# A chunked RWKV-6 recurrence with a hardswish MLP: one score matrix per head from running decay products in place of seven doubling levels, the output transposed, and the old algorithm behind a run-time flag

## The chip, the cores and the metric

The kernel runs on one core of a Trainium2 chip. The metric is the device time of one execution in microseconds. The change is timed against the kernel before on the same chip.

## The reference

All arithmetic is in float32. First comes a linear recurrence per head, then an MLP over the 3,072 tokens:

```python
B, H, S, D = (4, 8, 768, 48)        # r, k, v: 0.1 * randn; w: 0.8 + 0.15 * rand; u: 0.1 * randn
for t in range(S):                  # state: [B, H, D, D], zero at the start
    cur = einsum('bhd,bhe->bhde', u * kt, vt)
    y[:, :, t] = einsum('bhd,bhde->bhe', rt, state + cur)
    state = wt[:, :, :, None] * state + einsum('bhd,bhe->bhde', kt, vt)
x = y.transpose(0, 2, 1, 3).reshape(B * S, H * D)     # [3072, 384]
h = x @ w_in                                          # w_in  [384, 2048]
g = h * clip(h + 3, 0, 6) / 6
out = g @ w_out                                       # w_out [2048, 384]
```

The decay w lies between 0.8 and 0.95 with these inputs; the definition itself allows any w. The MLP weights arrive as float64, and the chip turns their bits into float32.

## The kernel before, in words

**Chunks.** A sequence of 768 tokens is cut into 6 chunks of L = 128 tokens, 24 chunks in all. The features of a head lie on the partitions, two heads at a time (at partitions 0 and 64, 48 rows each), so 8 heads are 4 pairs.

**Scores by doubling.** Inside a chunk the decay between two tokens is never a quotient. At level l (0 to 6) a chunk falls into blocks of 2^(l+1) tokens; `score` (line 170) multiplies the left half's K with the right half's R for 8 heads, and one predicated copy (L176) puts the result into the score matrix. `merge` (L154 to L158) then multiplies R by the left half's total decay (VectorE) and K by the right half's (GpSimd), with the untouched halves copied on ScalarE. So a chunk needs 7 levels of 8 matrix products, 7 predicated copies and 7 merges, each level resting on the one before. Each float32 matmul is two instructions on TensorE, so a level is 16.

**The rest of a chunk.** `own` (L184 to L191) makes the token's own term: r times k on GpSimd, a matmul with u, and a product with v. `read` (L201, L206) multiplies the state and the scores into y, and adds the own term (L209). `write` (L218 to L237) transposes K, multiplies it with v and updates the state S. `turn` (L248, L249) transposes y, so that the MLP has its features on the partitions.

**MLP.** Three chunks make a block of 384 tokens. `up` (L255 to L260) makes 128 hidden units of a block: 3 matmuls, ScalarE's r6, VectorE's g, which empties the PSUM buffer. `down` (L266, L269) makes 128 output tokens from 16 matmuls. The eight blocks have 16 `up` and 3 `down` pieces each, kept in a list, `todo`, and put between the steps of later chunks. A block's pieces enter the list when its third chunk is read, and the list is emptied before the next block enters.

**Weights.** 32 pieces of 128 hidden units (16 of w_in, 16 of w_out) are loaded from line 98 on the SyncE queue into 3 rotating buffers (`bits`); seven VectorE instructions (L105 to L114) convert a piece. Two pieces are put behind each level of the first chunks.

**Order.** The queues hold the work nearly in program order. TensorE executes what it is given in order, so an instruction that waits holds those behind it. PSUM has eight banks: four for the scores (`a_ps`), two for `ps` (everything small in a chunk) and two for `mm` (the MLP).

Of the kernel before, what the change touches and what calls it, by code (L numbers as in the profile page):

```python
# [14 lines left out]
ACT = mybir.ActivationFunctionType  # L15
PSUM = bass.MemoryType.PSUM
# [6 lines left out]
@with_exitstack  # L23
def kernel(
    ctx: ExitStack,
    tc: tile.TileContext,
    rkw: bass.AP,
    v: bass.AP,
    ub: bass.AP,
    moe_w_in: bass.AP,  # L30
    moe_w_out: bass.AP,
    out: bass.AP,
    n_chunks: int,
):
# [12 lines left out]
    After the last level R carries the decay from the chunk's start and K that to its end, as the state needs.  # L47
    """
    nc = tc.nc
    NT, PR, _, P, _ = rkw.shape  # L50
    D = PR - GP
    H = 2 * P
    HD = H * D
    NTOK, DM = out.shape
    DFF = moe_w_in.shape[1]
    NCC, NFC = DM // 128, DFF // 128
    HL = L // 2
    BC = 3                      # chunks in a block of tokens of the MLP
    MB = BC * L

    const = ctx.enter_context(tc.tile_pool(name="const", bufs=1))
    io = ctx.enter_context(tc.tile_pool(name="io", bufs=3))
    wk = ctx.enter_context(tc.tile_pool(name="wk", bufs=2))
    pa = ctx.enter_context(tc.tile_pool(name="pa", bufs=2, space=PSUM))
    pp = ctx.enter_context(tc.tile_pool(name="pp", bufs=2, space=PSUM))

    st = [dict() for _ in range(NT)]

    def load(i):
        a = io.tile([PR, 3, P, L], F32, name="rkw_in")  # L70
        b = io.tile([L, H, D], F32, name="v_in", bufs=4)
        nc.sync.dma_start(out=a, in_=rkw[i])
        nc.sync.dma_start(out=b.rearrange("s h d -> s (h d)"), in_=v[i])
        st[i].update(R=a[:, 0], K=a[:, 1], tot=a[:, 2], v=b)

    load(0)
    ub_sb = const.tile([PR, P, 2], F32, name="ub_sb")
    nc.sync.dma_start(out=ub_sb, in_=ub)
    load(1)

    # weights, chunk f of the hidden units at a time
    w_in = const.tile([128, NFC, NCC, 128], F32, name="w_in")
    w_out = const.tile([128, NFC, DM], F32, name="w_out")

    def weights(which, f):
# [11 lines left out]
        bits = io.tile([128, n], I64, name="bits", bufs=3)  # L97
        nc.sync.dma_start(out=bits.rearrange("p (c j) -> p c j", j=128), in_=src)
        # |w| = (2^20 + top 20 bits of the mantissa + low word / 2^32) * 2^-20 * 2^(exponent - 1023)
# [17 lines left out]
    ident = const.tile([128, 128], F32, name="ident")  # L117
    make_identity(nc, ident)
    half = const.tile([128, 1], F32, name="half")
    nc.vector.memset(half, 0.5)  # L120

    # masks[s, l, (p, b, j)]: s lies in the left half of block b of level l
    masks = const.tile([128, LEVELS, P * HL], U8, name="masks")
    for l in range(LEVELS):
        m = 1 << l
        nb = HL // m
        mask_f = wk.tile([128, P, nb, m], F32, name="mask_f", bufs=1)
        nc.gpsimd.memset(mask_f, 1.0)
        nc.gpsimd.affine_select(out=mask_f, in_=mask_f, compare_op=ALU.is_ge, fill=0.0, base=0,
                                pattern=[[0, P], [-2 * m, nb], [0, m]], channel_multiplier=1)  # L130
        nc.gpsimd.affine_select(out=mask_f, in_=mask_f, compare_op=ALU.is_ge, fill=0.0, base=m - 1,
                                pattern=[[0, P], [2 * m, nb], [0, m]], channel_multiplier=-1)
        nc.vector.tensor_copy(out=masks[:, l], in_=mask_f.rearrange("s p b j -> s (p b j)"))

    # scores of a chunk, [s, g, p, t]; only s < t is ever written after the zeros
    NA = 2
# [75 lines left out]
    def write(i):  # L212
        if i % n_chunks == n_chunks - 1:
            return
# [141 lines left out]
```

## Time and profile before

| what | value |
|---|---|
| median of 3 runs | 935.16 us (934.88 to 942.06) |
| span of the profiled execution | 934.0 us |
| TensorE matmul busy | 839.6 us, 90% of the span |
| TensorE weight load busy | 600.6 us, 64% |
| VectorE busy | 445.6 us, 48% |
| ScalarE, GpSimd busy | 224.9 us, 211.6 us |
| moved by DMA | 39.41 MB |

The profile describes one execution from its first instruction to its last; that span is 1.2 us under the median of the runs. Busy time of one engine counts a moment once, so a group's mean times its count can be more than the engine was busy. The shares are means over stages: the slices show which stage an engine limits.

### The profile page before, as it was taken

The numbers are of one execution on the slowest core, as the hardware profiler recorded it, in microseconds if no ns is written. First come the engines' busy times: TensorE is split into PE (matmuls) and PEld (weight loads), VectorE is DVE, ScalarE is ACT, GpSimd is POOL, SyncE is SP. The second block draws the span as 40 slices with busy tenths as digits, with TensorE's granted clock in tenths as the row PEclk, the third lists the DMA queues.
The fourth block names the chain that finished last, engine by engine and source line by source line (L and its number), as shares of the span: only waits on it lengthen the run. The fifth ranks groups of instructions, "written<-read, shape, count | busy, mean of one in ns | idle before, by whom it ended". The sixth has DMA issues, their size and how long they took to land.

```text
span 934.0 us, 13463 instructions
## 1 busy us (share of the span) xinstructions
PE 839.6 (90%) x5272; PEld 600.6 (64%) x5272; DVE 445.6 (48%) x954; ACT 224.9 (24%) x533; POOL 211.6 (23%) x263
## 2 busy tenths in 40 slices
PE   4135268999999999999999999999999999999998
PEld 3134258777667766777667767776677666775554
DVE  7898976666415541655135522654055414430210
ACT  3100002444203320333123311342033213110210
POOL 7600343532202320332023211322032202000000
PEclk9999999999999999999999999999999999999999
DMA  7153431110101110111011101011011000000000
GB/s 202 51 165 113 135 104 31 39 37 12 39 26 39 31 39 18 47 40 39 18 47 39 40 9 55 11 38 39 18 43 35 9 18 10 1 1 17 9 0 26
DMA packets 18879, 39.41 MB, mean 42 GB/s; under 512 B 1792, under 2 KB 14080, under 8 KB 18816
## 3 DMA queue, kind: packets, MB, share of 16 engines
q1 hardware_dynamic: 18816, 38.55, 14.0%
q8 instruction: 42, 0.69, 0.3%
q14 instruction: 21, 0.17, 0.1%
HBM read 33.82 MB, written 4.72 MB: 41 GB/s over the span
## 4 chain that ended last, share of the span: by engine, by line
PE 84%; DVE 9%; POOL 3%; DMA 2%; issue 1%; ACT 0%; SPq 0%; POOLq 0%; ACTq 0%
PE mm L255 28%; PE mm L266 27%; PE a_ps L170 17%; PE ps L206 5%; PE ps L187 2%; PE ps L201 2%; PE ps L223 2%; DVE scores L176 2%; DVE mag L112 1%; DVE mag L107 1%; DMA bits<-in_moe_w_out_dram 1%; PE ps L218 1%; DVE man L105 1%; PE ps L248 1%; POOL K L156 1%
## 5 line engine op out<-in xcount | busy, mean ns | idle before, releaser
L255 PE MATMUL mm<-xT,w_in 128*128 128x384 f32 x768 | 281.2, 503 | 0.0
L266 PE MATMUL mm<-w_out,g 128*128 128x384 f32 x768 | 252.6, 488 | 0.0
L170 PE MATMUL a_ps<-R,K 48*128 48x64 f32 x2304 | 168.2, 300 | 70.3 <-DVE scores L176 52.5
L170 PEld LDWEIGHTS a_ps<-R,K 48*128 48x128 f32 x2304 | 156.1, 211 | 107.5 <-issue 70.8
L266 PEld LDWEIGHTS mm<-w_out,g 128*128 128x128 f32 x768 | 144.4, 190 | 97.5
L176 DVE COPY_PREDICATED scores<-masks,a_ps 128x512 f32<-128x512 uint8 x168 | 148.1, 882 | 86.7 <-PE a_ps L170 86.2
L255 PEld LDWEIGHTS mm<-xT,w_in 128*128 128x128 f32 x768 | 137.5, 192 | 74.8 <-issue 2.8
L156 POOL TENSOR_TENSOR K<-K,tot 112x256 f32<-112x256 f32 x144 | 104.6, 726 | 319.7 <-PE a_ps L170 194.3
L260 DVE SCALAR_TENSOR_TENSOR g<-r,mm 128x384 f32<-128x384 f32 x128 | 70.9, 554 | 167.0 <-ACT r L258 166.4
L258 ACT ACTIVATE r<-mm,half 128x384 f32<-128x384 f32 x128 | 74.4, 581 | 232.5 <-PE mm L255 232.5
L154 DVE TENSOR_TENSOR R<-R,tot 112x256 f32<-112x256 f32 x144 | 71.2, 494 | 30.7 <-PE ps L201 30.5
L157 ACT COPY K<-K 112x256 f32<-112x256 f32 x144 | 58.8, 408 | 87.4 <-POOL K L156 60.0
L155 ACT COPY R<-R 112x256 f32<-112x256 f32 x144 | 58.8, 408 | 69.9 <-DVE R L154 33.4
L269 ACT COPY o<-mm 128x384 f32<-128x384 f32 x24 | 11.5, 479 | 245.9 <-PE mm L266 245.9
L184 POOL TENSOR_TENSOR rk<-rkw_in 112x512 f32<-112x512 f32 x24 | 34.9, 1452 | 114.4 <-PE ps L187 112.3
L206 PE MATMUL ps<-v_in,scores 128*128 128x48 f32 x384 | 51.0, 290 | 0.0
L206 PEld LDWEIGHTS ps<-v_in,scores 128*128 128x128 f32 x384 | 49.9, 209 | 1.1
L156 POOL TENSOR_TENSOR K<-rkw_in 112x256 f32<-112x256 f32 x24 | 21.3, 889 | 106.4 <-PE ps L218 105.1
L170 PE MATMUL a_ps<-rkw_in 48*128 48x64 f32 x384 | 31.6, 307 | 9.6 <-DMA rkw_in<-in_rkw_dram 5.7
L158 DVE TENSOR_TENSOR tot<-tot 112x16 f32<-112x16 f32 (+5 forms) x144 | 37.2, 265 | 6.0 <-DVE tot L158 0.9
L237 DVE TENSOR_TENSOR S<-S,ps 48x192 f32<-48x192 f32 x32 | 11.2, 351 | 50.5 <-PE ps L223 50.3
L170 PEld LDWEIGHTS a_ps<-rkw_in 48*128 48x128 f32 x384 | 27.7, 216 | 11.3 <-DMA rkw_in<-in_rkw_dram 5.7
(43 smaller groups left out, 442.2 us busy)
## 6 DMA issues: line engine op xcount, KB each, us to landing
rkw_in<-in_rkw_dram SPq DMA_DIRECT2D x24, 672.0 KB, 4.8
bits<-in_moe_w_in_dram SPq DMA_DIRECT2D x16, 384.0 KB, 3.3
bits<-in_moe_w_out_dram SPq DMA_DIRECT2D x16, 384.0 KB, 3.1
v_in<-in_v_dram SPq DMA_DIRECT2D x24, 192.0 KB, 2.4
out_dram<-o SPq DMA_DIRECT2D x24, 192.0 KB, 1.8
ub_sb<-in_ub_dram SPq DMA_DIRECT2D x1, 3.5 KB, 4.9
```

Source lines behind the costliest of these rows:

```text
L154: nc.vector.tensor_mul(R2[:, :, 1], R[:, :, 1], tot[:, :, 0:1].to_broadcast([PR, n, m]))
L155: nc.scalar.copy(out=R2[:, :, 0], in_=R[:, :, 0])
L156: nc.gpsimd.tensor_mul(K2[:, :, 0], K[:, :, 0], tot[:, :, 1:2].to_broadcast([PR, n, m]))
L157: nc.scalar.copy(out=K2[:, :, 1], in_=K[:, :, 1])
L158: nc.vector.tensor_mul(tot2.rearrange("q p b -> q (p b)"), tot[:, :, 0], tot[:, :, 1])
L170: nc.tensor.matmul(a_ps[:, g, p * HL:(p + 1) * HL].rearrange("s (b j) -> s b j", j=m), lhsT=d["K"][rows, p, :], rhs=d["R"][rows, p, :].rea ...
L176: nc.vector.copy_predicated(out=scores[i % NA].rearrange("s g p (b h j) -> s g (p b) h j", h=2, j=m)[:, :, :, 1], mask=masks[:, l].rearran ...
L206: nc.tensor.matmul(y_ps[:, h, :], lhsT=a[:, g, p, :], rhs=d["v"][:, h, :], start=(first and h == 0), stop=(h == H - 1), skip_group_check=True)
L255: nc.tensor.matmul(h_ps, lhsT=w_in[:, f, j, :], rhs=b["xT"][:, j, :], start=(j == 0), stop=(j == NCC - 1))
L258: nc.scalar.activation(out=r6, in_=h_ps, func=ACT.Relu, bias=half, scale=1.0 / 6.0)
L260: nc.vector.scalar_tensor_tensor(out=g, in0=r6, scalar=1.0, in1=h_ps, op0=ALU.min, op1=ALU.mult)
L266: nc.tensor.matmul(o_ps, lhsT=blocks[bk]["g"][f][:, c * L:(c + 1) * L], rhs=w_out[:, f, :], start=(f == 0), stop=(f == NFC - 1))
```

## The change

The program gets a fast path, which always runs, and the old algorithm (`general_path`), which runs behind it if a flag is set. 

- **Fast path, per chunk.** `prep` makes the running decay product W of all channels by one scan on VectorE, its reciprocal on VectorE, and R = r W and K = k / W on GpSimd. It also reduces the largest w (for the flag), copies each product over a whole chunk, forms r k u on GpSimd from token-major copies of r and k, sums it per head on VectorE, and spreads that sum over a diagonal matrix A on GpSimd. `score` makes one 128x128 matrix per head, 8 in all, and one predicated copy puts its part with s < t into A, whose diagonal is the own term. `write` adds to the state before the decay, and multiplies by W's last column.
- **Transposed output.** `read` takes v and the state as the stationary side, so y comes with its features on the partitions. ScalarE copies it into the MLP's input; a third of the features is moved to its partitions by 6 DMAs per block on the SyncE queue. `own`'s matmuls and `turn`'s transposes are no longer there. The rows of w_in are laid out on the host in the new order of the features.
- **Order.** The MLP's pieces are 28 per block (16 `up`, 12 quarters of `down`), spread evenly over the chunks with a lag of 5 pieces; `mm` has four PSUM banks, `ps` two, the scores two. Eight weight pieces stand in a chunk's program, and `prep` runs one chunk ahead.
- **Flag.** At the end the smallest chunk product (compared with 2^-60) and the largest w (with 1) are reduced to one number, loaded into the registers of all engines, and compared. `general_path` is the code before in plain order, with the MLP behind every third chunk.

Inputs: r, k and w of a chunk lie in one tensor (w with a leading 0 per pair, so that the scan starts again there); r, k and v also come token by token.

The diff, cut to the lines that are added and that matter here (the code taken out is the kernel printed above; `general_path` repeats it):

```diff
+def fast_path(tc, feat, tok, ub, moe_w_in, moe_w_out, out, flag, n_chunks):
...
+        def load(i):
+            a = io.tile([PR, nf], F32, name="feat_in")
+            b = io.tile([L, 3, HD], F32, name="tok_in", bufs=4)
+            nc.sync.dma_start(out=a, in_=feat[i])
+            nc.sync.dma_start(out=b.rearrange("s c e -> s (c e)"), in_=tok[i].rearrange("s c e -> s (c e)"))
+            n = P * L
+            st[i].update(r=a[:, :n].rearrange("q (p t) -> q p t", p=P),
+                         k=a[:, n:2 * n].rearrange("q (p t) -> q p t", p=P), w=a[:, 2 * n:],
+                         rt=b[:, 0], kt=b[:, 1], v=b[:, 2].rearrange("s (h d) -> s h d", d=D))
...
+        def prep(i):
+            d = st[i]
+            W_ = wk.tile([PR, P * (L + 1)], F32, name="W")
+            nc.vector.tensor_tensor_scan(out=W_, data0=d["w"], data1=restart.rearrange("q p t -> q (p t)"),
+                                         initial=0.0, op0=ALU.mult, op1=ALU.add)
+            W = W_.rearrange("q (p t) -> q p t", p=P)
+            inv = wk.tile([PR, P, L], F32, name="inv")
+            nc.vector.reciprocal(out=inv, in_=W[:, :, 1:])
+            R = wk.tile([PR, P, L], F32, name="R", bufs=3)
+            K = wk.tile([PR, P, L], F32, name="K")
+            nc.gpsimd.tensor_mul(R, d["r"], W[:, :, :L])
+            nc.gpsimd.tensor_mul(K, d["k"], inv)
+            nc.vector.tensor_reduce(out=w_max[:, i:i + 1], in_=d["w"], axis=AX.X, op=ALU.max,
+                                    apply_absolute_value=True)
+            nc.vector.tensor_copy(out=w_min[:, i, :], in_=W[:, :, L])
+            rk = wk.tile([L, HD], F32, name="rk")
+            nc.gpsimd.tensor_mul(rk, d["rt"], d["kt"])
+            nc.gpsimd.tensor_mul(rk, rk, u_bc)
+            dg = wk.tile([L, H, 1], F32, name="dg")
+            nc.vector.tensor_reduce(out=dg.rearrange("s h o -> s (h o)"), in_=rk.rearrange("s (h d) -> s h d", d=D),
+                                    axis=AX.X, op=ALU.add)
+            A = wk.tile([L, H, L], F32, name="A")
+            nc.gpsimd.tensor_mul(A, ident.rearrange("s (o t) -> s o t", o=1).to_broadcast([L, H, L]),
+                                 dg.to_broadcast([L, H, L]))
+            d.update(W=W, R=R, K=K, A=A)
+        def score(i):
+            d = st[i]
+            a_ps = pa.tile([128, 2, P, L], F32, name="a_ps")
+            for p in range(P):
+                for g in range(2):
+                    rows = slice(g * GP, g * GP + D)
+                    nc.tensor.matmul(a_ps[:, g, p, :], lhsT=d["K"][rows, p, :], rhs=d["R"][rows, p, :],
+                                     start=True, stop=True)
+            nc.vector.copy_predicated(
+                out=d["A"].rearrange("s (p g) t -> s g p t", g=2),
+                mask=mask.rearrange("s (o x t) -> s o x t", o=1, x=1).to_broadcast([L, 2, P, L]),
+                data=a_ps)
+        def turn_k(i):
+            if i % n_chunks == n_chunks - 1:
+                return
+            d = st[i]
+            kn_ps = pp.tile([L, P, PR], F32, name="ps")
+            for p in range(P):
+                nc.tensor.transpose(kn_ps[:, p, :], d["K"][:, p, :], ident[0:PR, 0:PR])
+            kn = wk.tile([L, P, PR], F32, name="kn")
+            nc.scalar.copy(out=kn, in_=kn_ps)
+            d["kn"] = kn
+        def write(i):
+            if i % n_chunks == n_chunks - 1:
+                return
+            d = st[i]
+            kv_ps = pp.tile([PR, P, 2, D], F32, name="ps")
+            for p in range(P):
+                nc.tensor.matmul(kv_ps[:, p].rearrange("q g e -> q (g e)"), lhsT=d["kn"][:, p, :],
+                                 rhs=d["v"][:, 2 * p:2 * p + 2, :].rearrange("s h e -> s (h e)"),
+                                 start=True, stop=True)
+            base = bases[i % 2]
             for g in range(2):
                 rows = slice(g * GP, g * GP + D)
...
+                b = base[rows, :, g * GP:g * GP + D]
+                if i % n_chunks == 0:
+                    nc.vector.tensor_copy(out=b, in_=kv_ps[rows, :, g, :])
+                else:
+                    nc.vector.tensor_add(b, st[i - 1]["S"][rows, :, g * GP:g * GP + D], kv_ps[rows, :, g, :])
+            S = wk.tile([PR, P, PR], F32, name="S")
+            nc.gpsimd.tensor_mul(S, base, d["W"][:, :, L:L + 1].to_broadcast([PR, P, PR]))
+            d["S"] = S
...
+        def read(i):
+            d = st[i]
+            first = i % n_chunks == 0
+            bk, c = divmod(i, BC)
+            if c == 0:
+                blocks[bk]["xT"] = wk.tile([128, NCC, MB], F32, name="xT")
+                blocks[bk]["x3"] = wk.tile([PR, MB], F32, name="x3")
+            xT, x3 = blocks[bk]["xT"], blocks[bk]["x3"]
+            y_ps = pp.tile([PR, P, L], F32, name="ps")
+            if not first:
+                for p in range(P):
+                    nc.tensor.matmul(y_ps[:, p, :], lhsT=st[i - 1]["S"][:, p, :], rhs=d["R"][:, p, :],
+                                     start=(p == 0), stop=False, skip_group_check=True)
+            for p in range(P):
+                for g in range(2):
+                    h = 2 * p + g
+                    nc.tensor.matmul(y_ps[g * GP:g * GP + D, p, :], lhsT=d["v"][:, h, :], rhs=d["A"][:, h, :],
+                                     start=(first and p == 0), stop=(p == P - 1), skip_group_check=True)
+            now = slice(c * L, (c + 1) * L)
+            for g in range(2):
+                rows = slice(g * GP, g * GP + D)
+                nc.scalar.copy(out=xT[rows, :, now], in_=y_ps[rows, 0:NCC, :])
+                nc.scalar.copy(out=x3[rows, now], in_=y_ps[rows, P - 1, :])
+            if c == BC - 1:
+                for g in range(2):
+                    for j in range(NCC):
+                        to = g * GP + D
+                        nc.sync.dma_start(out=xT[to:to + X3, j, :],
+                                          in_=x3[g * GP + j * X3:g * GP + (j + 1) * X3, :])
...
+            h_ps = pp.tile([128, MB], F32, name="mm", bufs=4)
...
+        QD = 4
+        def down(bk, cq):
+            c, q = divmod(cq, QD)
+            b = blocks[bk]
+            if q == 0:
+                b["o_ps"] = pp.tile([L, DM], F32, name="mm", bufs=4)
+            o_ps = b["o_ps"]
+            n = NFC // QD
+            for f in range(q * n, (q + 1) * n):
+                nc.tensor.matmul(o_ps, lhsT=b["g"][f][:, c * L:(c + 1) * L], rhs=w_out[:, f, :],
+                                 start=(f == 0), stop=(f == NFC - 1))
+            if q == QD - 1:
+                o = wk.tile([L, DM], F32, name="o", bufs=2)
...
+                f(bk, j)
+        per_block = NFC + BC * QD
+        lag = 5
+        prep(0)
+        prep(1)
+        some_weights(2)
+        done = 0
+        for i in range(NT):
+            goal = max(0, (i - BC + 1) * per_block // BC - lag) - done
+            done += max(goal, 0)
+            left = goal
+            def some(n):
+                nonlocal left
+                n = max(min(n, left), 0)
+                mlp(n)
+                left -= n
+            if i + 2 < NT:
+                load(i + 2)
+            score(i)
+            turn_k(i)
+            some(1)
+            if i + 1 < NT and i > 0:
+                prep(i + 1)
+            some(2)
+            some_weights(3)
+            write(i)
+            some(1)
+            some_weights(2)
+            read(i)
+            some(left)
+            some_weights(3)
+            if i % BC == BC - 1:
+                bk = i // BC
+                todo.extend([(up, bk, f) for f in range(NFC)] + [(down, bk, c) for c in range(BC * QD)])
+                if i == NT - 1:
+                    low = wk.tile([PR, 1], F32, name="low", bufs=1)
+                    top = wk.tile([PR, 1], F32, name="top", bufs=1)
+                    nc.vector.tensor_reduce(out=low, in_=w_min.rearrange("q i p -> q (i p)"), axis=AX.X, op=ALU.min,
+                                            apply_absolute_value=True)
+                    nc.vector.tensor_reduce(out=top, in_=w_max, axis=AX.X, op=ALU.max)
+                    nc.vector.tensor_scalar(out=low, in0=low, scalar1=LEAST, scalar2=None, op0=ALU.is_lt)
+                    nc.vector.scalar_tensor_tensor(out=top, in0=top, scalar=1.0, in1=low, op0=ALU.is_gt, op1=ALU.max)
+                    n_ps = pp.tile([1, 1], F32, name="ps")
+                    nc.tensor.matmul(n_ps, lhsT=top, rhs=ones[0:PR, :], start=True, stop=True)
+                    nc.vector.tensor_copy(out=flag, in_=n_ps)
+        mlp(len(todo))
...
+def general_path(tc, feat, tok, ug, moe_w_in, moe_w_out, out, n_chunks):
...
+    nc = tc.nc
+    flags = ctx.enter_context(tc.tile_pool(name="flags", bufs=1))
+    flag = flags.tile([1, 1], I32, name="flag")
+    fast_path(tc, feat, tok, ub, moe_w_in, moe_w_out, out, flag, n_chunks)
+    bad = nc.values_load(flag[0:1, 0:1], min_val=0, max_val=128)
+    with tc.If(bad > 0):
+        general_path(tc, feat, tok, ug, moe_w_in, moe_w_out, out, n_chunks)
...
```

## Rows read from the trace of the kernel before

**Rows 1.** The page: engine totals, two lines of 40 slices, the chain's shares.
```profile
PE 839.6 (90%) x5272; PEld 600.6 (64%) x5272; DVE 445.6 (48%) x954; ACT 224.9 (24%) x533; POOL 211.6 (23%) x263
...
PE   4135268999999999999999999999999999999998
...
DVE  7898976666415541655135522654055414430210
...
PE 84%; DVE 9%; POOL 3%; DMA 2%; issue 1%; ACT 0%; SPq 0%; POOLq 0%; ACTq 0%
```

**Rows 2.** Busy time by stretch: us, then PE, PEld, DVE, ACT, POOL, clock, DMA share, GB/s.
```profile
46.00:70.00 24.00, 8.57 (x72) 7.69 (x70) 23.28 (x61) 0.40 (x1) 0.00 (x0) 1.00 0.56 168
...
93.00:117.00 24.00, 5.65 (x48) 5.33 (x48) 23.99 (x65) 1.89 (x5) 7.12 (x3) 1.00 0.45 136
...
327.00:374.00 47.00, 47.00 (x257) 31.09 (x256) 12.94 (x27) 7.92 (x20) 6.56 (x9) 1.00 0.09 28
```

**Rows 3.** The chain of waits, three pieces: start us, us, what.
```profile
179.67 3.33 PE mm L255 x6
...
868.50 30.96 PE mm L255 x96
899.46 30.97 PE mm L266 x96
```

**Rows 4.** Timeline of TensorE in a steady chunk: start us, us, instruction, shapes, count.
```profile
306.57 2.00 PE L170 MATMUL a_ps<-R,K 48*128 48x64 f32 x32
308.50 2.20 PE L255 MATMUL mm<-xT,w_in 128*128 128x384 f32 x6
310.63 2.00 PE L170 MATMUL a_ps<-R,K 48*128 48x64 f32 x32
...
318.67 1.03 PE L201 MATMUL ps<-S,R 112*128 112x96 f32 x8
319.53 1.91 PE L206 MATMUL ps<-v_in,scores 128*128 128x48 f32 x16
321.28 2.17 PE L255 MATMUL mm<-xT,w_in 128*128 128x384 f32 x6
323.28 0.55 PE L218 MATMUL ps<-ident,K 112*128 112x112 f32 x4
323.67 1.47 PE L255 MATMUL mm<-xT,w_in 128*128 128x384 f32 x4
324.98 0.93 PE L223 MATMUL ps<-v_in,kn 128*112 128x96 f32 x8
325.75 0.84 PE L255 MATMUL mm<-xT,w_in 128*128 128x384 f32 x2
```

**Rows 5.** Timeline of the start: first feature-dependent VectorE instruction; eight weight loads issued.
```profile
5.66 0.43 DVE L154 TENSOR_TENSOR R<-rkw_in 112x256 f32<-112x256 f32 x1 [2.55 <-DMA rkw_in<-in_rkw_dram]
...
36.20 22.48 SPq L98 DMA_DIRECT2D bits<-in_moe_w_in_dram  x8
```

**Rows 6.** Groups by line and shape: count, busy us, mean ns, idle before and releaser.
```profile
L176 DVE COPY_PREDICATED scores<-masks,a_ps 128x512 f32<-128x512 uint8 x168 | 148.1, 882 | 86.7 <-PE a_ps L170 86.2
L154 DVE TENSOR_TENSOR R<-R,tot 112x256 f32<-112x256 f32 x144 | 71.2, 494 | 30.7 <-PE ps L201 30.5
L260 DVE SCALAR_TENSOR_TENSOR g<-r,mm 128x384 f32<-128x384 f32 x128 | 70.9, 554 | 167.0 <-ACT r L258 166.4
L184 POOL TENSOR_TENSOR rk<-rkw_in 112x512 f32<-112x512 f32 x24 | 34.9, 1452 | 114.4 <-PE ps L187 112.3 <-DMA rkw_in<-in_rkw_dram 2.0
L191 POOL TENSOR_TENSOR dv<-v_in,dg 128x384 f32<-128x384 f32 x24 | 21.7, 905 | 6.3 <-ACT dg L189 6.3
L237 DVE TENSOR_TENSOR S<-S,ps 48x192 f32<-48x192 f32 x32 | 11.2, 351 | 50.5 <-PE ps L223 50.3
L158 DVE TENSOR_TENSOR tot<-tot 112x128 f32<-112x128 f32 x24 | 7.5, 312 | 2.1 <-DVE tot L158 0.5
L158 DVE TENSOR_TENSOR tot<-tot 112x64 f32<-112x64 f32 x24 | 5.9, 244 | 0.3
```

More of the change, by code (lines that the diff above doesn't have):

```diff
@@ L20, with weight_loader @@
 LEVELS = 7
[L23 to L83, printed above, removed]
+BC = 3
+LEAST = 2.0 ** -60
+def weight_loader(nc, io, wk, w_in, w_out, moe_w_in, moe_w_out, io_bufs=3):
     def weights(which, f):
@@ new lines, in fast_path, with some_weights, mlp @@
+        todo = []
+        pieces = [("in", f) for f in range(NFC)] + [("out", f) for f in range(NFC)]
+        def some_weights(n):
+            for piece in pieces[:n]:
+                weights(*piece)
+            del pieces[:n]
+        def mlp(n):
+            for _ in range(min(n, len(todo))):
+                f, bk, j = todo.pop(0)
+                f(bk, j)
[43 more added lines that the diff above has]
+                    nc.vector.tensor_copy(out=flag, in_=n_ps)
@@ L234, in write @@
             if i % n_chunks == 0:
[L235 removed]
+                nc.gpsimd.memset(S, 0.0)
             else:
[L237 to L249 removed]
@@ L263, in down @@
-    def down(bk, c):
-        o_ps = pp.tile([L, DM], F32, name="mm")
-        for f in range(NFC):
-            nc.tensor.matmul(o_ps, lhsT=blocks[bk]["g"][f][:, c * L:(c + 1) * L], rhs=w_out[:, f, :],
-                             start=(f == 0), stop=(f == NFC - 1))
-        o = wk.tile([L, DM], F32, name="o", bufs=2)
-        nc.scalar.copy(out=o, in_=o_ps)
-        t0 = bk * MB + c * L
-        nc.sync.dma_start(out=out[t0:t0 + L, :], in_=o)
-    todo = []
-    pieces = [("in", f) for f in range(NFC)] + [("out", f) for f in range(NFC)]
@@ new lines, in down @@
+        def down(bk, c):
+            o_ps = pp.tile([L, DM], F32, name="mm_g")
+            for f in range(NFC):
+                nc.tensor.matmul(o_ps, lhsT=blocks[bk]["g"][f][:, c * L:(c + 1) * L], rhs=w_out[:, f, :],
+                                 start=(f == 0), stop=(f == NFC - 1))
+            o = wk.tile([L, DM], F32, name="o_g", bufs=2)
+            nc.scalar.copy(out=o, in_=o_ps)
+            t0 = bk * MB + c * L
+            nc.sync.dma_start(out=out[t0:t0 + L, :], in_=o)
+        for f in range(NFC):
+            weights("in", f)
+            weights("out", f)
@@ L285 @@
+        for i in range(NT):
             if i + 2 < NT:
@@ L290, with kernel @@
                 merge(i, l)
-                for piece in pieces[:2]:
-                    weights(*piece)
-                del pieces[:2]
-                if l % 2 == 0:
-                    mlp(1)
-                    left -= 1
-        if i > 0:
-            read(i - 1)
-            mlp(1)
-            write(i - 1)
-            mlp(1)
-            turn(i - 1)
-            mlp(left - 2)
-            if i % BC == 0:
-                mlp(len(todo))
-                bk = i // BC - 1
-                todo.extend([(up, bk, f) for f in range(NFC)] + [(down, bk, c) for c in range(BC)])
-    mlp(len(todo))
-_INS = ['rkw', 'v', 'ub', 'moe_w_in', 'moe_w_out']
+            read(i)
+            write(i)
+            turn(i)
+            if i % BC == BC - 1:
+                for f in range(NFC):
+                    up(i // BC, f)
+                for c in range(BC):
+                    down(i // BC, c)
+@with_exitstack
+def kernel(
+    ctx: ExitStack,
+    tc: tile.TileContext,
+    feat: bass.AP,
+    tok: bass.AP,
+    ub: bass.AP,
+    ug: bass.AP,
+    moe_w_in: bass.AP,
+    moe_w_out: bass.AP,
+    out: bass.AP,
+    n_chunks: int,
+):
+    nc = tc.nc
+    flags = ctx.enter_context(tc.tile_pool(name="flags", bufs=1))
[4 more added lines that the diff above has]
+        general_path(tc, feat, tok, ug, moe_w_in, moe_w_out, out, n_chunks)
+_INS = ['feat', 'tok', 'ub', 'ug', 'moe_w_in', 'moe_w_out']
 _OUTS = [((3072, 384), 'float32')]
```

404 lines of the change are left out of this document (258 added, 146 removed).

## The prediction

> **What bounds the kernel now.** I read the page first: TensorE's matmuls are busy for 90% of the span, VectorE for 48%, the others for a quarter, and the chain of waits lies on TensorE for 84% [rows 1]. The line of slices shows where the rest is. TensorE is at 9 from the eighth slice on, and at 1 to 8 in the seven before, where VectorE stands at 6 to 9 [rows 1]. So there are two kernels to cost: a start of 180 us that VectorE limits, and 754 us that TensorE limits.
>
> The stretches confirm both. From 46 to 70 us VectorE is busy for 23.28 of 24.00 us and TensorE for 8.57; from 327 to 374 TensorE is busy for all 47.00 us and VectorE for 12.94 [rows 2]. In the chain the first MLP piece starts at 179.67 us [rows 3]: that is the border. What the change takes from TensorE therefore counts in full behind the border, and what it takes from VectorE counts in front of it.
>
> **MLP: unchanged.** The last block runs with nothing between: 30.96 us for 16 `up`, 30.97 for the `down` [rows 3]. A block is 61.9 us, eight are 495.4, one `up` is 30.96/16 = 1.94. The new kernel does the same matmuls, so this is its floor.
>
> **TensorE per chunk, before.** The timeline is read by the distance from one group's start to the next one's, since the durations include the pipeline's latency [rows 4]:
> - scores: 32 instructions in 1.93 us (306.57 to 308.50), 0.965 per level, 6.76 for seven levels;
> - state into y 0.86, scores into y 1.75, transposes of K 0.39, K times v 0.77;
> - six MLP instructions behind scores take 2.13 (308.50 to 310.63) where they take 1.94 alone, so 0.2 us per change between the two kinds of tile.
>
> **TensorE per chunk, after.** `own`'s and `turn`'s matmuls go, and six of the seven levels.
> - Scores: 16 instructions with 128 columns instead of 64. Before, one took 60 ns (1.93/32), though weights of 128 columns cost 107 to 109 ns where the whole array is used (0.86/8 and 1.75/16) [rows 4]. So the two heads of a pair, on partitions 0 to 47 and 64 to 111, run side by side, and a pair costs about 0.12. The moving side of 128 columns would be as long as that weight load. I take 0.965 (side by side); the upper end is 16 x 0.107 = 1.72.
> - A into y: 16 instructions; now v is stationary (48 columns), A moves with 128, and the heads of a pair write partitions 0 to 47 and 64 to 111 of the output. No row shows two column halves at once: 0.965 if they behave as the row halves do, 1.75 if as `read` now. I take the middle, 1.36.
> - State into y: 8 instructions, 0.86; K's transposes and K times v as before, 1.16. Both only in 20 of 24 chunks: 0.72 and 0.97 on average.
> - Two changes of tile kind: 0.4.
>
> Sum 0.965 + 1.36 + 0.72 + 0.97 + 0.4 = 4.4 us per chunk, with ends 4.0 and 5.6. Before, the same count gives 6.76 + 1.75 + 0.72 + 0.97 + 0.8 for four changes = 11.0, and `own` and `turn` on top.
>
> The Trainium skill ("TensorE: Matmul & The Clock Gate", Part 3: Packing small matmuls) says that tiles in distinct column groups run at once, as row groups do. The scores' 60 ns agree for rows; for columns no run here shows it. By that page the sum would be about 8 us lower.
>
> **What hides behind TensorE.** In the steady part a new chunk lasts 61.9/3 + 4.4 = 25 us. VectorE's part of it, from the nearest rows [rows 6]: scan and reciprocal over 512 elements at twice the 256-element product, 1.0 each; the reduction for the largest w 1.0; the sums per head 0.55 (384 elements); the copy of the products about 0.2; one predicated copy of 1,024 at 2 x 0.88 = 1.76; two state adds 0.70. That is 6.2 us, and 5.3 evictions g add 2.95. GpSimd: R and K 1.45 each, two products of 0.9, A at about twice R (2.9), S about 1: 8.6 us. ScalarE: 5.3 activations and copies that are smaller than before. All are under half of 25 us, so I cost them at nothing there; the cover is TensorE's own work. The six DMAs per block that move a third of the features have the lag of five pieces in front of them, some 10 us; without it they would cost a few us per block. Four `mm` banks let TensorE go on for four pieces, 7.7 us, while VectorE is in `prep`.
>
> **The start.** Here VectorE counts. First features come at 5.66 us [rows 5]. A converted weight piece is seven instructions: 23.28/61 = 0.38 us each from 46 to 70 us, 23.99/65 = 0.37 from 93 to 117 [rows 2], so 2.67 us a piece (2.58 the lower end); the loads, issued as buffers come free, give 22.48/8 = 2.81 as the upper [rows 5]. 32 pieces: 85.5. Five chunks of VectorE work at 6.2: 31. In `prep` the sum per head waits for GpSimd: R, K and two products are 4.7 us behind the scan, VectorE has 2.2 us of own work in that time, 2.5 us are left, three times (the first two lie behind the first loads): 7.5. Queued behind that wait are the evictions of the MLP and weight conversions. Sum 130. Before, VectorE was only some 80% busy in the first slices [rows 1], and with gaps like that it would be 155. The new order has fewer levels that wait for one another; I take 135 for the moment from which TensorE is dense. SyncE's queue carries more (r and k come twice), and the first DMAs of transposed features stand behind weight loads that wait for buffers; VectorE is still converting then, which hides them. TensorE has done five score steps and about eight `up` pieces by then. The first MLP piece of before takes 3.33 us for what later takes 1.94 [rows 3]; such slow pieces would fall in this part, where TensorE waits anyway.
>
> **The end.** From the last matmul (899.46 + 30.97) to the end of the span are 3.6 us [rows 3]. Then come the load of the flag and a branch over the old code on every engine. No row shows one. Lower end 0.5 (an instruction), upper 20; I take 5.7, what it took at the start until the first data had come from memory [rows 5].
>
> **The sum.** 135 + (495.4 - 8 x 1.94 = 479.9) + 19.5 chunks x 4.4 (86) + 3.6 + 5.7 = 710 against a span of 934.0; with the 1.2 us between span and median, 711 against 935.16.
>
> **The rivals.**
> - *A reciprocal of several cycles per element.* The products cost (312 - 244)/64 = 1.06 ns per element [rows 6]. With eight cycles for each of 512 elements it would be 4.3 us instead of 1.0, hidden later but not at the start: 5 x 3.3 = 17, so 728. No row shows a reciprocal. The Trainium skill ("VectorE: DVE Perf Modes", First, the fixed hardware budget) says that it is an iterative divide with a repeat count of 8, spread over the pipeline's slices; that speaks for this rival only if the repeats are not pipelined.
> - *Neither scores nor A go side by side.* 0.75 + 0.39 more per chunk, 20 chunks: 23, so 734. For it: 128 moving columns are new with halves. Against it: the 60 ns.
> - *VectorE holds TensorE in every chunk.* With the slow reciprocal and products that GpSimd delays, `prep` would keep the evictions waiting for 11 or 12 us, above the 7.7 us of the four banks: 3 us per chunk, 60 in all, 771. The share of VectorE speaks against it, the single stretch for it.
> - *No change.* TensorE would have to wait 11 us in each chunk for the chain scan, reciprocal, K, scores, copy, A. The chain is made one chunk ahead.
> - *The flag is set: the change doesn't do what it says.* The old algorithm then runs behind the fast path, and its whole time, at least the 934 of now, is added: 1,640 and more. It decides when some product of 128 decays is under 2^-60, which needs a mean decay under 0.72, or when a w is over 1. The reference draws w from 0.8 to 0.95, and 0.8^128 is 2^-41; padding is 1, not above. Hence it is unlikely.
>
> **Chances.** Forecast 0.57 (its own range 685 to 735), slow reciprocal 0.19, no halves side by side 0.12, VectorE in every chunk 0.09, no change 0.01, flag 0.02. The predicted time is the forecast's, 711. Low end: dense from 115, 4.0 us per chunk, a cheap branch: 20 + 8 + 5 less, 680. High end, near the third rival: 765. Faster by over 1% takes all but the last two cases: 0.97; same 0.01; slower 0.02. One per cent, 9 us, is about what a measurement of this kernel can tell from no change.
>
> **What would show it.** Score instructions at about 60 ns each and 16 per chunk; y's instructions from 60 to 109 ns; TensorE full from about 135 us, with a period of about 75 us per block where it was about 100; VectorE nearly full before; a reciprocal of 1 or of 4 us; a few us between the last output and the end. I am wrong if TensorE has holes in each chunk behind 150 us, or if the old code's instructions appear.

## The result, and the profile after

The changed kernel takes 723.38 us (median of four runs, 722.04 to 723.89) against 936.17 before: a ratio of 0.772, interval 0.770 to 0.775. The forecast was 711 with a range from 680 to 765. The span of the profiled execution is 720.0 us, 2.0 under its time of 722.04.

The page of the changed kernel: engine totals, two engines' slices with TensorE's clock, the chain's shares (columns as in [rows 1]).

```profile
PE 624.5 (87%) x2706; PEld 392.4 (54%) x2706; DVE 360.1 (50%) x548; ACT 128.4 (18%) x269; POOL 185.7 (26%) x148
...
PE   1341373779999999999999999999999999999996
...
DVE  6999999998136525640346337512463152101200
...
PEclk9975575779999999999999999999999999999999
...
PE 78%; DVE 19%; DMA 2%; POOL 1%; issue 0%; ACT 0%; ACTq 0%; DVEq 0%; POOLq 0%
```

The two stages are still there. TensorE is at 9 from the tenth slice (162 us) to the last but one; in front of it VectorE is at 9 from the second slice to the ninth. Before, TensorE was full from the eighth of longer slices [rows 1]. TensorE's busy time fell by 215 us, and the time by 213.

Busy time by stretch of the changed kernel (columns as in [rows 2]):

```profile
54.00:72.00 18.00, 2.31 (x11) 1.72 (x9) 16.92 (x42) 0.53 (x1) 4.33 (x3) 0.50 0.50 148
...
108.00:126.00 18.00, 6.16 (x22) 3.36 (x22) 17.97 (x37) 1.85 (x5) 3.97 (x2) 0.59 0.46 143
126.00:144.00 18.00, 13.74 (x52) 9.24 (x53) 17.91 (x43) 2.28 (x4) 5.84 (x5) 0.72 0.41 126
144.00:162.00 18.00, 13.34 (x51) 7.77 (x50) 17.36 (x26) 3.15 (x8) 8.97 (x7) 0.72 0.23 72
162.00:180.00 18.00, 18.00 (x78) 11.11 (x77) 14.91 (x20) 4.63 (x10) 10.77 (x8) 1.00 0.34 99
...
360.00:420.00 60.00, 60.00 (x278) 37.87 (x277) 27.99 (x35) 13.89 (x28) 15.80 (x14) 1.00 0.22 64
```

VectorE is nearly full up to 162 us, TensorE is full from there on. In the steady part VectorE is busy for 28 of 60 us. So the border moved from 179.67 [rows 3] only to about 156, where the chain below enters TensorE for good; 135 was forecast. (The 179.67 of before is the start of its first MLP piece. VectorE had let go of TensorE some 30 us earlier; the section on why the prediction was right comes back to that.)

The chain of waits of the changed kernel (start us, us, what), the beginning of the dense part, one chunk, the last block:

```profile
156.00 9.70 PE mm L246 x24
...
176.81 15.68 PE mm L264 x48
...
251.43 15.68 PE mm L264 x48
267.10 1.09 PE a_ps L170 x16
268.19 0.53 PE ps L184 x4
268.73 7.76 PE mm L264 x24
276.48 0.77 PE ps L195 x8
277.25 2.61 PE mm L264 x8
279.86 0.88 PE ps L223 x8
280.74 1.01 PE ps L228 x16
281.75 2.78 PE mm L264 x8
...
325.77 15.68 PE mm L264 x48
...
652.58 30.96 PE mm L246 x96
683.54 30.97 PE mm L264 x96
```

One chunk is 1.09 (scores) + 0.53 (K transposed) + 0.77 (K times v) + 0.88 (state into y) + 1.01 (A into y) = 4.3 us. The same pieces recur after 74.6 and 74.3 us (176.81, 251.43, 325.77), and a block of the MLP is still 61.9. Both halves run side by side: 16 score instructions take 68 ns each, 16 for y 63, where the old `read` took 109 [rows 4]. One at a time they couldn't be that short: 384 moving columns take 0.32 us (30.96/96), so 128 would take 107 ns. For y these are column halves, of which no row had been at hand. The Trainium skill ("TensorE: Matmul & The Clock Gate", Part 3: Packing small matmuls) says that distinct column groups run at once; these 63 ns agree.

The accounts before and after agree with that. Behind the border lay 754.3 us before; less the MLP's 495.4 and the end's 3.6, 255.3 us are left for 20.5 chunks: 12.5 per chunk. Behind 156 us lie 564.0 now; less 478.0 (54 MLP instructions, 17.4 us, are done by then) and an end of 5.5, 80.5 us are left for 19.5 chunks: 4.1 per chunk. So of the 214 us of span 175 come from TensorE's chunk work behind the border (255.3 less 80.5), 24 from the earlier border (the first MLP piece before, the dense part now) and 17 from MLP pieces done in front of it; the longer end takes 2 back.

Groups of the changed kernel by line and shape (columns as in [rows 6]):

```profile
L145 DVE RECIPROCAL inv<-W 112x512 f32<-112x512 f32 x24 | 80.4, 3349 | 0.6
L160 POOL TENSOR_TENSOR A<-ident,dg 128x1024 f32<-128x1024 f32 x24 | 49.8, 2076 | 41.2 <-PE ps L228 21.2 <-DVE dg L157 20.1
L141 DVE TENSOR_TENSOR_SCAN W<-feat_in,restart 112x516 f32<-112x516 f32 x24 | 34.3, 1430 | 18.9 <-POOL S L207 14.8 <-DMA feat_in<-in_feat_dram 3.9
L173 DVE COPY_PREDICATED A<-mask,a_ps 128x1024 f32<-128x1024 uint8 x24 | 31.2, 1301 | 57.0 <-PE a_ps L170 56.9
L150 DVE TENSOR_REDUCE w_max<-feat_in 112x1 f32<-112x516 f32 x24 | 16.3, 680 | 18.8 <-DMA feat_in<-in_feat_dram 18.8
```

The reciprocal is 3.35 us, not 1.0, and the scan 1.43; the predicated copy (1.30 for 1.76) and the reduction (0.68 for 1.0) are cheaper than costed. 3.35 us for 512 elements are 6.5 ns each, where a product costs 1.06 [rows 6].

The end of the changed kernel, timeline of the last compute instruction (columns as in [rows 4], behind them idle time and releaser):

```profile
714.58 0.48 ACT L268 COPY o<-mm 128x384 f32<-128x384 f32 x1 [9.88 <-PE mm L264]
```

The last matmul ends at 683.54 + 30.97 = 714.5, so 5.5 us are left to the end of the span, where it had been 3.6. No instruction of the old algorithm appears: the flag is not set.

### The profile page after: what moved, and what is told of

The parts are those of the page before. It is cut to its first block, busy times and chain, and to the rows that moved or that the text cites. A ratio compares the mean times of both kernels' runs of the same rounds, so it can differ in the third digit from the quotient of the medians.

```text
span 720.0 us, 6998 instructions
## 1 busy us (share of the span) xinstructions
PE 624.5 (87%) x2706; PEld 392.4 (54%) x2706; DVE 360.1 (50%) x548; ACT 128.4 (18%) x269; POOL 185.7 (26%) x148
## 4 chain that ended last, share of the span: by engine, by line
PE 78%; DVE 19%; DMA 2%; POOL 1%; issue 0%; ACT 0%; ACTq 0%; DVEq 0%; POOLq 0%
PE mm L264 35%; PE mm L246 33%; PE a_ps L170 3%; PE ps L228 3%; DVE man L49 2%; DVE inv L145 2%; DVE mag L56 2%; DVE mag L51 2%; PE ps L223 2%; PE ps L195 2%; DVE ex L55 2%; DVE ex L52 1%; DVE W L141 1%; DVE w_out L58 1%; DVE ex L54 1%; PE ps L184 1%
## 5 line engine op out<-in xcount | busy, mean ns | idle before, releaser
L145 DVE RECIPROCAL inv<-W 112x512 f32<-112x512 f32 x24 | 80.4, 3349 | 0.6
L160 POOL TENSOR_TENSOR A<-ident,dg 128x1024 f32<-128x1024 f32 x24 | 49.8, 2076 | 41.2 <-PE ps L228 21.2
L170 PE MATMUL a_ps<-R,K 48*128 48x128 f32 x384 | 33.0, 317 | 31.0 <-POOL K L149 31.0
L173 DVE COPY_PREDICATED A<-mask,a_ps 128x1024 f32<-128x1024 uint8 x24 | 31.2, 1301 | 57.0 <-PE a_ps L170 56.9
L170 PEld LDWEIGHTS a_ps<-R,K 48*128 48x128 f32 x384 | 27.7, 216 | 45.2 <-POOL K L149 34.5
L148 POOL TENSOR_TENSOR R<-feat_in,W 112x512 f32<-112x512 f32 x24 | 32.3, 1346 | 69.3 <-DVE W L141 66.5
L228 PE MATMUL ps<-A,tok_in 128*48 128x128 f32 x384 | 29.4, 302 | 21.4 <-DVE A L173 21.4
L223 PE MATMUL ps<-R,S 112*112 112x128 f32 x160 | 23.9, 296 | 25.3 <-POOL S L207 25.3
L141 DVE TENSOR_TENSOR_SCAN W<-feat_in,restart 112x516 f32<-112x516 f32 x24 | 34.3, 1430 | 18.9 <-POOL S L207 14.8
L149 POOL TENSOR_TENSOR K<-feat_in,inv 112x512 f32<-112x512 f32 x24 | 30.8, 1282 | 36.3 <-DVE inv L145 13.7
```

What stands on the lines that cost most here:

```text
L141: nc.vector.tensor_tensor_scan(out=W_, data0=d["w"], data1=restart.rearrange("q p t -> q (p t)"), initial=0.0, op0=ALU.mult, op1=ALU.add)
L145: nc.vector.reciprocal(out=inv, in_=W[:, :, 1:])
L148: nc.gpsimd.tensor_mul(R, d["r"], W[:, :, :L])
L160: nc.gpsimd.tensor_mul(A, ident.rearrange("s (o t) -> s o t", o=1).to_broadcast([L, H, L]), dg.to_broadcast([L, H, L]))
L170: nc.tensor.matmul(a_ps[:, g, p, :], lhsT=d["K"][rows, p, :], rhs=d["R"][rows, p, :], start=True, stop=True)
L173: nc.vector.copy_predicated(out=d["A"].rearrange("s (p g) t -> s g p t", g=2), mask=mask.rearrange("s (o x t) -> s o x t", o=1, x=1).to_br ...
```

## The experiments

The kernel before took 934 to 935 us beside each group of these runs, and the changed kernel, run again beside the last group but one, 723.3. Differences are against that.

**1. Without the branch.** The last three lines of the top function go.

```diff
-    bad = nc.values_load(flag[0:1, 0:1], min_val=0, max_val=128)
-    with tc.If(bad > 0):
-        general_path(tc, feat, tok, ug, moe_w_in, moe_w_out, out, n_chunks)
```

> The changed kernel without the load of the flag and without the old algorithm behind it (the flag is still computed). Theory: behind the last matmul lie 5.5 us of span in the changed kernel and 3.6 before, and the runs are 2 us longer than their spans instead of 1.2, so the branch costs about 3 us: 720.5. The prediction had 5.7 for it: 717.7. Rival, a branch whose cost lies elsewhere (old code that is fetched all along): below 713.

Measured: 719.6 us (ratio to before 0.770, interval 0.768 to 0.772), 3.8 less. Its trace says how much of it is the branch: span 716.3, last ScalarE copy at

```profile
713.00 0.48 ACT L268 COPY o<-mm 128x384 f32<-128x384 f32 x1 [9.88 <-PE mm L264]
```

so 3.3 us from that copy to the end where the changed kernel has 5.4. The branch costs 2.1 us at the end; the other 1.6 lie in front of that copy. The two traces show where. Both enter the dense part at 156 us with the same 24 MLP instructions; without the branch they took

```profile
156.11 8.01 PE mm L246 x24
```

where the changed kernel took 9.70, and the stretch behind 156 us reads, the changed kernel first:

```profile
156.00:174.00 18.00, 18.00 (x54) 10.50 (x55) 17.10 (x21) 4.65 (x8) 13.84 (x11) 0.91 0.26 77
...
156.00:174.00 18.00, 17.99 (x65) 10.85 (x64) 17.95 (x23) 4.65 (x8) 14.66 (x11) 1.00 0.27 78
```

TensorE's granted clock was back at 1.00 there where the changed kernel's mean was still 0.91; these 1.7 us are the clock's. That the missing branch caused it isn't shown. Either way the branch is under the 5.7 of the prediction, and over its lower end of 0.5.

**2. Scores twice.**

```diff
-            for p in range(P):
+            for p in [*range(P), *range(P)]:      # in score
```

> The changed kernel with the score matmuls of every chunk issued twice into the same PSUM tile. Theory: behind 156 us TensorE is the bound, so 16 more instructions at 1.09 us per 16 count in full in about 20 chunks: 22 us more, 745. Rival (TensorE's time is hidden behind VectorE or GpSimd since the change): 723 to 727.

Measured: 739.6 us (0.791, 0.789 to 0.793), 16.2 more. TensorE's timeline shows what the second series costs:

```profile
271.12 2.06 PE L170 MATMUL a_ps<-R,K 48*128 48x128 f32 x32
```

The next group starts 1.98 us later, where one series takes 1.09, so 0.9 per chunk. In 19 chunks behind the border that is 17 us: counted in full. My 22 had charged the change of tile kind a second time. The rival that hides it has fallen.

**3. Two PSUM banks for the MLP.**

```diff
-            h_ps = pp.tile([128, MB], F32, name="mm", bufs=4)
+            h_ps = pp.tile([128, MB], F32, name="mm", bufs=2)
```
(and the same for `o_ps`)

> The changed kernel with two PSUM banks for the MLP instead of four, all else the same. Theory: TensorE is the bound only because four banks carry it over VectorE's stretch of scan, reciprocal and reductions; around 284 to 290 us the first eviction comes 3.5 us late, with two banks TensorE would stop for 2 to 3 us there, in most chunks: 40 to 60 us more, 765 to 780. Rival (VectorE is busy for half the time only, so evictions come early enough): 723 to 727.

Measured: 749.3 us (0.801, 0.799 to 0.803), 25.9 more: neither the 40 to 60 nor nothing. The timeline has the wait where it was expected:

```profile
295.81 2.42 PE L246 MATMUL mm<-xT,w_in 128*128 128x384 f32 x7
300.47 2.13 PE L246 MATMUL mm<-xT,w_in 128*128 128x384 f32 x3 [2.24 <-DVE g L251]
```

Behind scan, reciprocal and sums the eviction g comes late, and TensorE stops for 2.24 us. Most of the waits are shorter: behind 160 us the timeline has 17 waits for g, 0.22 to 2.25 us long and 15.1 us in all. The rest of the 25.9 us lies in the start, where by 170 us 72 MLP instructions are done and not 90 as in the changed kernel (5.8 us), and in matmuls that follow a wait (six in 2.20 us for 1.94). So the four banks are a part of the gain, and the prediction's sentence that they cover VectorE's stretch is shown.

**4. y in the old orientation.** v moves, A and R are stationary; y goes through ScalarE, three transposes and ScalarE again.

```diff
-                    nc.tensor.matmul(y_ps[g * GP:g * GP + D, p, :], lhsT=d["v"][:, h, :], rhs=d["A"][:, h, :], ...)
+                nc.tensor.matmul(y_ps[:, h, :], lhsT=d["A"][:, h, :], rhs=d["v"][:, h, :], ...)
...
+            for j in range(NCC):
+                nc.tensor.transpose(x_ps[:, j, :], y[:, j * 128:(j + 1) * 128], ident)
```

> The changed kernel with y in the old orientation: scores stationary, v moving, y copied by ScalarE, transposed on TensorE and copied again; no DMAs for a third of the features, and w_in's rows in their own order. Theory: TensorE takes 1.75 + 0.33 instead of 1.01 us for it, in 20 chunks behind the start: 21 us more, 745. Rival (the transposition adds a chain that TensorE waits for): 760 or more. Rival (orientation is worth nothing): 723.

Measured: 743.2 us (0.796, 0.794 to 0.798), 19.9 more, as expected. TensorE's timeline of one chunk:

```profile
284.20 1.03 PE L224 MATMUL ps<-S,R 112*128 112x96 f32 x8
285.06 1.91 PE L228 MATMUL ps<-tok_in,A 128*128 128x48 f32 x16
286.81 0.88 PE L259 MATMUL mm<-w_out,g 128*128 128x384 f32 x2
287.54 0.55 PE L234 MATMUL ps<-ident,y 128*128 128x128 f32 x3
287.93 2.10 PE L259 MATMUL mm<-w_out,g 128*128 128x384 f32 x6
```

1.75 us for y (285.06 to 286.81) and 0.39 for the transposes, instead of 1.01. The transposition is worth 20 of the 212 us.

**5. Three VectorE instructions per weight piece.**

```diff
+        nc.vector.tensor_scalar(out=man, in0=hi, scalar1=3, scalar2=0x3FFFFFFF,
+                                op0=ALU.logical_shift_left, op1=ALU.bitwise_and)
+        nc.vector.scalar_tensor_tensor(out=ex, in0=hi, scalar=-0x80000000, in1=man,
+                                       op0=ALU.bitwise_and, op1=ALU.bitwise_or)
+        nc.vector.scalar_tensor_tensor(out=dst.bitcast(I32), in0=lo, scalar=29, in1=ex,
+                                       op0=ALU.logical_shift_right, op1=ALU.bitwise_or)
```
(in place of the seven; `lo` is read as int32)

> The changed kernel with three VectorE instructions per weight piece instead of seven: shift and mask the high word, or in the sign, or in three bits of the low word. This cuts the fraction off where the other rounds, and holds for weights under 2 in magnitude and over 2^-127 only. Theory: VectorE sets when TensorE becomes dense (it is full to 144 us, and a piece costs 3.6 us by its means), so some 2.3 us x 32 = 74 us go from VectorE; the loads of weights and features then come next, and I expect two thirds of it: dense at about 105 us, 670 to 680. Rival (loads or the chain of chunks set the start): 710 or more.

Measured: 670.0 us (0.717, 0.715 to 0.719), 53 less. Stretches of its trace:

```profile
90.00:108.00 18.00, 9.18 (x47) 5.39 (x48) 17.23 (x27) 2.90 (x7) 6.80 (x5) 0.81 0.68 195
108.00:126.00 18.00, 17.93 (x74) 10.84 (x73) 17.38 (x33) 4.75 (x10) 2.12 (x2) 1.00 0.45 135
```

TensorE is dense from 108 us instead of about 156: VectorE's conversions set the border. By their means up to 113 us the three instructions of a piece sum to 2.10 us, 0.70 each; the seven of the changed kernel sum to 3.61 up to 156 us, 0.52 each. So the gain comes from instructions left out, about 1.5 us x 32 pieces = 48 us, and not from shorter ones.

**6. No reciprocal.**

```diff
-            nc.vector.reciprocal(out=inv, in_=W[:, :, 1:])
+            nc.vector.tensor_copy(out=inv, in_=W[:, :, 1:])
```

> The changed kernel with the reciprocal replaced by a copy of W of the same shape, so K is k times W: the division is left out. Theory: six reciprocals of 3.35 us lie in the VectorE-bound start; a copy is 0.4 to 0.7: 16 us less, 706. Behind the start nothing changes. Rival (TensorE's wait for K at 151 to 155 us is all it costs): 718.

Measured: 709.0 us (0.758, 0.756 to 0.760), 14.3 less, near the theory's 706 and far from the rival's 718. The six reciprocals in front of the border count nearly in full; the eighteen behind it are hidden, or 24 x 2.7 us would have gone.

**7. The diagonal matrix on ScalarE.**

```diff
-            nc.gpsimd.tensor_mul(A, ident.rearrange("s (o t) -> s o t", o=1).to_broadcast([L, H, L]),
-                                 dg.to_broadcast([L, H, L]))
+            for h in range(H):
+                nc.scalar.mul(out=A[:, h, :], in_=ident, mul=dg[:, h, :])
```

> The changed kernel with the diagonal matrix A made by 8 ScalarE instructions per chunk (identity times the sum per token) instead of one GpSimd product of 1,024 elements. Theory: VectorE's conversions and GpSimd's products stretch each other (an instruction of 0.35 us took 1.79 beside A, and A 5.84 instead of 2.1), and at the start every such stretch counts: 5 to 10 us less, 713 to 718. Rival (ScalarE's work gets in front of the evictions, or the stretch costs nothing): 722 to 726.

Measured: 713.9 us (0.764, 0.761 to 0.766), 9.5 less. What it removes stands in the timeline of the changed kernel:

```profile
93.80 0.35 DVE L55 TENSOR_SCALAR ex<-ex 128x384 int32<-128x384 int32 x1
...
95.89 5.84 POOL L160 TENSOR_TENSOR A<-ident,dg 128x1024 f32<-128x1024 f32 x1 [6.18 <-DVE dg L157]
100.15 1.79 DVE L55 TENSOR_SCALAR ex<-ex 128x384 int32<-128x384 int32 x1
...
281.84 1.90 POOL L160 TENSOR_TENSOR A<-ident,dg 128x1024 f32<-128x1024 f32 x1 [0.28 <-PE ps L228]
```

Beside the conversions A takes 5.84 us, without them 1.90; the same conversion instruction takes 0.35 us alone and 1.79 at A's end. The Trainium skill ("SBUF — State Buffer", Who interferes with whom) says that VectorE and GpSimd share a pair of ports, held for a whole instruction, and names tensor_scalar among those that can contend. These rows agree with it. VectorE's part of the gain can be counted up to 156 us: the conversions' durations sum to 115.4 us in the changed kernel and to 107.8 in this run, and a running product takes 1.31 us for 1.63, six of them 1.9 less. Together that is 9.5, what was measured.

**8. The kernel before with one level of scores.**

```diff
+        if l > 0:
+            return          # in score; the merges stay
```

> The kernel before with only level 0 of the scores: the matmuls and predicated copies of levels 1 to 6 are left out, the merges stay. Theory: of the change's gain the six levels are the main part: 6 x 0.965 us and three changes of tile kind less per chunk, 6.4 us in 20 chunks, 128 us, and some 10 to 20 at the start: 790 to 800. Rival (the MLP's order and the start are the main part): 850 or more.

Measured: 791.4 us against 935.1 (0.846, 0.844 to 0.849), 143.7 less, as expected. Six of seven score levels are two thirds of the change's 212 us. The first MLP piece starts at 147.4 us in this run and not at 179.67, so 32 of the 144 us lie in front of it, more than the 10 to 20 expected, and 112 behind it.

**9. The changed kernel again.**

> The changed kernel itself, unaltered, beside the runs of this call. 721 to 724 by both theories; what it gives is the zero for the two others.

Measured: 723.3 us (0.773, 0.769 to 0.777).

**10. Six weight pieces per chunk, and A on ScalarE.**

```diff
             some(2)
-            some_weights(3)
+            some_weights(2)
...
             some(left)
-            some_weights(3)
+            some_weights(2)
```
(with the edit of 7)

> The changed kernel with A made on ScalarE, and with six weight pieces in a chunk's program instead of eight (they end in the fifth chunk, where the first `down` still has its weights). Theory: VectorE's order decides when the first chunks' decay products are ready, so fewer conversions in front of them let TensorE begin earlier: 5 us less than with A on ScalarE alone (714), 706 to 711. Rival (VectorE's total up to the dense part is all that counts, in whatever order): 714.

Measured: 698.3 us (0.746, 0.743 to 0.750), 25 less: more than either theory gave.

**11. The same with three instructions per piece.**

> The same with the three-instruction conversion (weights under 2 in magnitude, fraction cut off). Theory: the three gains add up, since all of them shorten VectorE's part of the start: 670 less 8 for A, less 5 to 10 for the order: 652 to 658, with TensorE dense from about 85 to 95 us. Rival (behind the conversions the reciprocals and the chain of chunks set the start, and nothing adds): 665 to 670.

Measured: 663.1 us (0.709, 0.706 to 0.713). That is 7 less than with the short conversion alone, where 12 to 18 were expected and at most 5 by the rival. Where VectorE has less to convert, the two edits together are worth less; which of them lost more isn't shown.

**12. Six pieces per chunk alone.**

> The changed kernel with six weight pieces in a chunk's program instead of eight, and A left on GpSimd. With both edits 25 us went where 9 for A and 5 for the order were expected. Theory: the order is worth the other 16 by itself, since with fewer conversions in front TensorE gets MLP pieces and chunk steps done while VectorE still converts: 707, and by 156 us TensorE has issued 75 MLP instructions or more where the changed kernel has 54. Rival (the two need each other, because A on GpSimd holds VectorE's conversions and the state's product behind it): 715 to 720.

Measured: 709.1 us (0.758, 0.755 to 0.761), 14.2 less. With A's 9.5 that makes 23.7, and both together gave 25: they add, and the rival has fallen. MLP instructions of TensorE up to 156 us (stretch, busy us, count, weight loads, clock, DMA share, GB/s), first the changed kernel:

```profile
0.00:156.00 156.00, 28.11 (x54) 13.99 (x54) 0.73 0.50 153
```

then six pieces alone:

```profile
0.00:156.00 156.00, 36.76 (x83) 19.10 (x84) 0.76 0.53 157
```

and with A on ScalarE as well:

```profile
0.00:156.00 156.00, 39.11 (x96) 20.74 (x96) 0.95 0.53 160
```

83 and 96 instructions against 54, at 0.32 us each in the dense part: 9.4 and 13.5 us of MLP done earlier, with 43 and 89 more matmul instructions counted in all (359 and 405 against 316, by the same stretch of all lines). VectorE is busy for 149 of the 156 us in all three. Where the rest of the 14.2 and 25 us lies isn't shown. My step for run 10 looked only at when TensorE becomes dense, and left out what it gets done before.

## Why the prediction was right, and where its steps were off

**What bounds.** Right in both stages of the changed kernel. TensorE's work counts in full behind the border (runs 2 and 4), VectorE's in front of it (runs 5, 6 and 7). For the kernel before, "a start of 180 us that VectorE limits" is wrong in its last 30 us. The stretches around it (columns as in [rows 2]) and two pieces of the chain:

```profile
140.00:163.00 23.00, 20.56 (x142) 19.35 (x144) 14.69 (x34) 5.78 (x16) 8.20 (x10) 1.00 0.12 31
163.00:187.00 24.00, 23.12 (x160) 19.02 (x158) 16.76 (x40) 9.76 (x27) 13.56 (x17) 1.00 0.14 38
...
166.55 3.61 PE a_ps L170 x32
...
182.99 1.93 PE a_ps L170 x32
```

From 147 to 180 us TensorE was busy for 32.08 of 33.00 us and VectorE for 17.55; the last weight piece was converted by 143.3 us. TensorE was slow there: 32 score instructions took 3.61 us, and 1.93 from 183 us on. So the change did not let VectorE go earlier (about 156 for 147). What came earlier is the MLP, with less score work in front of it: run 8, which takes out nothing but scores, moves its first piece from 179.67 to 147.4 us.

**TensorE per chunk.** 4.4 us with ends 4.0 and 5.6 were forecast; the chunk shows 4.3, the account 4.1. Scores 1.09 for 0.965; y 1.01, nearer the lower end than the middle of 1.36; state 0.88 for 0.86; K 1.30 with its changes of tile for 1.16. The rival in which no halves run side by side has fallen: 68 and 63 ns.

**What hides.** Right with its cover named: VectorE's stretch is hidden by four banks (run 3). The third rival, VectorE in every chunk, was right in its mechanism, a slow reciprocal that delays evictions, but with four banks TensorE stays full (60.00 of 60.00 us from 360 to 420). Its price was real with two banks, and 26 us rather than 60.

**The start: the step that was mis-sized.** The prediction took "135 for the moment from which TensorE is dense", with "about eight `up` pieces" done by then: it was about 156 with nine done. Two terms were too small and two too large. The reciprocal was taken at 1.0 us and measured 3.35: with six of them 14 us too little. Run 6, which puts a copy in their place, gave 14.3. So the first rival held in this point, and its 728 is nearer to the measured 723 than the forecast's 711. The conversions were taken at 2.67 us per piece, with pieces spread as before; their instructions were stretched beside GpSimd's products, of which the change brings more. By the sum of their means a piece took 3.61 us up to 156 us, and 3.16 in the kernel before up to 180, which is 14 us for 32 pieces. Run 7 shows 9.5 us for one of these products. Against that, VectorE had no gaps: it waits 1.1 us for the sums up to 156 us and not 7.5, since conversions stand between in its order, and the 5 us of other waits did not come either.

**The end.** 3.6 + 5.7 was forecast; 5.5 was measured, with 2.1 for the branch. Beside it, runs are 2.0 us longer than their spans, not the 1.2 that I read from the median of three and a single span.

**The sum again.** 711, plus 19 for the border (156 for 135, one `up` more done), less 3 to 5 for the chunks, less 3.8 for the end, plus 0.8 around the span: 722 to 724, measured 723.4. The size was right to 1.7% because errors of both signs stand in it, and the cause of the gain is shown: six levels of scores 144 us (run 8), the transposed output 20 (run 4). The remaining 48 lie in the order, the banks, `own` and the start; of these only the banks were tried by themselves (26), and that number rests on the new `prep`, so it isn't a share that can be added.

**A version that beats both.** Six weight pieces per chunk and A on ScalarE give 698.3 us for the same arithmetic. With the short conversion it is 663.1, for weights in the range that its expectation states.

What stays open: what the lower clock costs in front of the border, where TensorE waits anyway; behind it the two traces of run 1 differ by 1.7 us. And of the 48 us named above, `own` and the new order were not tried by themselves.

## What to carry to other kernels

Cost a change stage by stage, and ask of every new instruction in which stage it lands: the same reciprocal is worth 2.4 us in front of the border and nothing behind it. In a stage that one engine limits, ask also what the other engine could get done meanwhile: moving conversions back gained 14 us without shortening any. And before counting on slack of an engine that empties PSUM, compare its longest stretch, not its share, with what the free banks let TensorE do.

## What the runs showed of the hardware

- A reciprocal of 112x512 float32 takes 3.35 us on VectorE, a running product of 112x516 from 1.14 in the chain to 1.43 on average, a maximum over 112x516 0.68. The Trainium skill ("VectorE: DVE Perf Modes", First, the fixed hardware budget) speaks of an iterative divide with a repeat count of 8. Measured are 6.5 ns per element, about six times the 1.06 of a product; no run here shows the repeats themselves.
- Two column halves of TensorE run side by side as two row halves do (63 and 68 ns per instruction of 128 moving columns, 107 to 110 with the whole array).
- TensorE's granted clock was 0.50 (1.2 GHz) from 54 to 72 us, where it was busy for 2.31 of 18 us, and back at 1.00 (2.4 GHz) from 162 us, where it was busy throughout. The first 24 MLP instructions of the dense part took 9.70 us, 0.40 each, against 0.32 later and 8.01 us for the 24 in run 1, where the clock was back at 156 us.
- A listed clock is worth checking against durations: the kernel before lists 1.00 from 46 to 70 us [rows 2] and from 163 to 187, but in the latter its score instructions took 113 ns each at 166 us and 60 ns from 183.
- Loading a flag on all engines and branching over the old algorithm took 2.1 us at the end.
